# The third-weight output of two token groups as one Strassen step, transposed, instead of two plain accumulations

## The chip, the cores and the metric

One core of a Trainium2 chip runs the whole program in one launch. The metric is the device time of that launch in microseconds. Engines: TensorE (PE) multiplies 128x128 stationary blocks by moving blocks of up to 512 columns into PSUM, VectorE (DVE), ScalarE (ACT) and GpSimd (POOL) do the elementwise work, SyncE (SP) issues most DMAs.

## The reference

Two batches of 768 tokens with 8 heads of 64 pass through a decayed linear attention, then through two feed-forward blocks, all in float32:

```python
x = attn_out.transpose(0, 2, 1, 3).reshape(1536, 512)
h = x @ w_in                       # 512 -> 2048
x = np.maximum(0.01 * h, h) @ w_out   # 2048 -> 512
a = x @ w1                         # 512 -> 1024
b = x @ w2                         # 512 -> 1024
out = ((a * b) @ w3) @ w_out2      # 1024 -> 1024 -> 512
```

## The kernel before, in words

The 1536 tokens form three groups of 512 (`T`, `NG`). Each float32 operand of a product is split into a rounded high half and the rest (`hi` on ScalarE, `lo` on VectorE or GpSimd, both in `halves_of`, L821), and each product is three matmuls (`EXACT`: high-high, low-high, high-low). `w3` and the last weight are multiplied with each other first (`unit_w`, L1044); the result `w34` (1024 x 512, eight slices of 128 rows) is kept in two float32 tiles. This is the "third weight" of the title.

The last part of the program works on eight slices of the inner dimension F (1024 = 8 x 128). For the first group, `unit_ab` makes a slice of a*b and `unit_o` (L1280) multiplies it by its slice of `w34`. For the second and third group together, `unit_pair` (L964) makes a and b of a slice by one Strassen step: seven products of 6 matmuls each (p1 to p7, L981) into three PSUM banks, with copies on ScalarE (`keep`, L993) and adds and multiplications on VectorE (`dve`, L997) between them. The operands that come from the weights are made for each slice in `pair_weights` (L930): four 256-wide sums and four splits. The results: m0 is a*b of the second group, m1 that of the third. m0 is split at once (`pair_ops`, L691); m1 is stored and split later (`stored_pair`, L1035).

The output of those two groups is plain. `unit_o(1, f)` runs between the products of the next pair, `unit_o(2, f)` after the last pair. In each, for 4 chunks of 128 tokens, the chunk of a*b is the stationary operand and the slice of `w34` (512 columns) the moving one, three products each, accumulated over the eight slices (`accumulate`, L728, matmuls at L689, banks `acc` for the second group, `ps` for the third). The pieces of `w34` are split anew for each group, in the ring `wy`. At the end each 128 x 512 result is copied to a tile `f` and stored; the very last copy is done in two halves by VectorE and ScalarE.

The order of all engines is fixed when the program is built. `in_order` (L65) holds every operation with a cost, a rank, what it comes after and which buffers it takes and uses; each time an engine is free it gives it the operation of lowest rank among those that are ready. A buffer belongs to a ring of a few slots (`RINGS`), and a take waits for the users of the slot's former owner. An operation with `port=True` on VectorE and any on GpSimd are never planned at the same time. `both` (L834) is one elementwise operation of VectorE or GpSimd on two SBUF operands, `WIDE` for 512 columns.

Of the kernel before, what the change touches and what calls it, by code (L numbers as in the profile page):

```python
# [20 lines left out]
T = 512  # L21
# [103 lines left out]
def tile_kernel(ctx: ExitStack, tc, qkv, lamb, w_in, w_out, w1, w2, w3t, wo, out):  # L125
# [4 lines left out]
    RINGS = {  # L130
# [3 lines left out]
    }  # L134

    TAGS = {"yf0": ("yf0",), "yf1": ("yf1",), "yf2": ("yf2",)}
# [1 line left out]
    TAGS["sd"] = ("wide0", "wide1", "more0", "more1")  # L138
    TWO = {
        "sx": (("w34_4", "w34_5"), ("w34_6", "w34_7"), ("old0", "old1"), ("old2", "old3")),  # L140
        "wy": tuple((f"w34_{2 * i}", f"w34_{2 * i + 1}") for i in range(4)),
    }
    FIXED = (
        "raw", "rp", "rn", "u", "f", "wi", "wp", "wx", "xy", "inp", "act", "qd", "kd", "a", "yf0", "yf1", "yf2", "sx",
        "wy", "sd",
    )
    pools = {
        r: ctx.enter_context(tc.tile_pool(name=r, bufs=n, **({"space": PS} if r in ("ps", "acc") else {})))
# [12 lines left out]
    def new(buf, shape, dtype=F32):  # L161
        tags = TAGS.get(buf.ring, (buf.ring,))
        turn[buf.ring] = turn.get(buf.ring, -1) + 1
        if buf.ring in TWO:
            tags = TWO[buf.ring][turn[buf.ring] % 4]
# [158 lines left out]
    def weight(kind, i, g, rank):  # L324

        if (kind, i) in pairs:
            return pairs[kind, i]
        if kind == "w34":
            get, last, fb = (lambda: w34[i // 4][:, i % 4, :]), kept_op[kind, i], []
        elif (kind, i) in kept_op:  # L330
            get, last, fb = (lambda: kept[i].tile[int(kind == "w2")]), kept_op[kind, i], [kept[i]]
        else:
            get, last, fb = convert(kind, i, rank)
            if kind in ("w1", "w2"):
                kept_op[kind, i] = last
        two = kind == "w34" and g > 0
        buf = Buf("wy" if two else "wi" if kind == "in" or kind == "wo" and i < 6 else "wp")
# [3 lines left out]
        if two and g == 1 and i < 4:  # L341
            order += kept[i].users

        def split(e):
            new(buf, [P, 512] if two else [P, 2, 512], F32R)
            hi(lambda: part(0), get)(e)

        part = (lambda v: buf.tile[v]) if two else (lambda v: buf.tile[:, v, :])
# [3 lines left out]
        o2 = op(  # L352
            {"dve": 680} if len(pairs) < 4 else {"dve": 680, "pool": 1250}, lo(lambda: part(1), lambda: part(0), get),
            rank, [o1], [],
            [*fb, *takes, *uses], port=True,
        )
        if kind in ("in", "out"):
# [4 lines left out]
    wo_buf, wo_part = {}, {}  # L362

# [359 lines left out]
        gp[g, f] = pair_ops(o1, ps, rank_next)  # L723

    yf, yf_ops, ys, y_ops = {}, {}, {}, {}
    held = []

    def accumulate(tag, g, f, nf, rank, w_ops, bufs, job, pairs, evac):  # L728

        if f % nf == 0:  # L730
            accs[tag, g] = [Buf("ps" if tag == "o" and g == NG - 1 else "acc") for _ in range(4)]
        acc = accs[tag, g]
        first = f % nf == 0
        after = [*w_ops, *([] if first else [acc_op[tag, g]])]
# [6 lines left out]
                products([(acc[c].tile, *job(c)) for c in cs], pairs, first, last)  # L741
            return fn

        if tag == "o" and g == NG - 1 and f == nf - 2:

            held.append((after, bufs, job))
            return
        if first and g == NG - 1:
            for c in range(4):
                after.append(op({"pe": 680}, mm([c], False), rank, after, [acc[c]], bufs, behind=after[-1:]))  # L750
            acc_op[tag, g] = after[-1]
            return
        if tag == "o" and g == 1 and f == nf - 2:
            for k in range(2):
                after.append(op({"pe": 1360}, mm([2 * k, 2 * k + 1], False), rank + 16 * k, after, [], [*acc, *bufs]))
            acc_op[tag, g] = after[-1]
            return
        if f % nf < nf - 1:
# [4 lines left out]
        two = [*held] if tag == "o" else []  # L763
        for after2, bufs2, _ in two:
            after, bufs = [*after, *after2], [*bufs, *bufs2]
        for c in range(4):
            def steps_of(e, c=c, fn=mm([c], True)):
                for _, _, job2 in two:
                    products([(acc[c].tile, *job2(c))], pairs, False, False)
                fn(e)  # L770

            o = op({"pe": 680 * (1 + len(two))}, steps_of, rank, after, [], [acc[c], *bufs])
            evac(c, acc[c], o)

    def unit_y(g, f, rank):
# [183 lines left out]
        quarters(("a22",), w2f(1), [last], w, n)  # L959
        return st  # L960

    stored, through, store_buf = {}, {}, {}

    def unit_pair(f, rank):  # L964

# [34 lines left out]
                takes, uses,  # L1000
            )

        p1 = product(0, b1, "a11", "b11", [], through[f - 1][:1] if f else ())
        t1, s1 = keep("ta", b1, p1)
        p7 = product(5, b3, "s3", "t3", [], through[f - 1] if f else ())
        p6 = product(10, b1, "s2", "t2", [p1, s1])
# [4 lines left out]
        t4, k4 = keep("ta", b1, p5)  # L1011
        r22 = Buf("tb")
        c22 = dve(lambda: new(r22, [P, T]), lambda: b3.tile, lambda: t4.tile, ALU.add, [p7, k4], [r22], [b3, t4])
        p3 = product(35, b1, "s4", "b22", [p5, k4])

        if f % 2 == 0:
            store_buf[f // 2] = Buf("wi")
        sb = store_buf[f // 2]

        def store():  # L1020
            if f % 2 == 0:
                new(sb, [P, 2, T])
            stored[f] = sb.tile[:, f % 2, :]
            return stored[f]

        m1 = dve(store, lambda: b1.tile, lambda: r22.tile, ALU.mult, [p3, c22], [] if f % 2 else [sb], [b1, r22, *([sb] if f % 2 else [])])
        p4 = product(40, b3, "a22", "t4", [p7, c22])
        through[f] = p2, p3, p4
        r21 = Buf("ta")
        c21 = dve(lambda: new(r21, [P, T]), lambda: b3.tile, lambda: u2.tile, ALU.add, [p4, k2], [r21], [b3, u2])  # L1030
        m0 = dve(lambda: b2.tile, lambda: b2.tile, lambda: r21.tile, ALU.mult, [c11, c21], [], [b2, r21])
        abp[1, f] = pair_ops(m0, b2, soon)
        kept_op["ab", f] = m1

    def stored_pair(f, rank):  # L1035

        buf = Buf("act")
        ops_ = halves_of(
            lambda v: buf.tile[:, v, :], lambda: stored[f], [kept_op["ab", f]], [buf], [store_buf[f // 2]], rank,
            lambda: new(buf, [P, 2, T], F32R),  # L1040
        )
        abp[2, f] = buf, ops_

    def unit_w(f, rank, rank_next):  # L1044
        halves = [weight("w3", 2 * f + j, 0, rank) for j in range(2)]
# [234 lines left out]
    def unit_o(g, f, rank):  # L1280
# [4 lines left out]
        def evac(c, acc, o):  # L1285
            fb = Buf("f")
            r0 = g * T + c * P

            def fn(e):
                copy = nc.scalar.copy if e == "act" else nc.vector.tensor_copy  # L1290
                copy(new(fb, [P, DM]), acc.tile)

            if g == NG - 1 and c == CPG - 1:

                def part(k):
                    def half_fn(e):
                        if k == 0:
                            new(fb, [P, DM])
                        copy = nc.scalar.copy if e == "act" else nc.vector.tensor_copy
                        w = slice(k * DM // 2, (k + 1) * DM // 2)  # L1300
                        copy(fb.tile[:, w], acc.tile[:, w])  # L1301
                        (nc.scalar if k else nc.sync).dma_start(out=out[r0 : r0 + P, w], in_=fb.tile[:, w])
                    return half_fn

                op0 = op({"dve": 300}, part(0), rank, [o], [fb], [acc])
                op({"act": 300}, part(1), rank, [o], [], [acc, fb], behind=[op0])
                return
# [77 lines left out]
        unit_o(0, f, r(f) + 20)  # L1385
    rank = r(NF2)
    pair_late(rank - 40)
    r = lambda f: rank + 45 * f
    for f in range(NF2):
        if f == NF2 - 1:  # L1390
            stored_pair(0, r(f))
        unit_pair(f, r(f))
        if f:
            unit_o(1, f - 1, r(f) + 25)
    unit_o(1, NF2 - 1, r(NF2) + 15)
    for f in range(NF2):
        if f:
            stored_pair(f, r(NF2) + 10 * f)
        unit_o(2, f, r(NF2) + 20 + 10 * f)

    with tc.manual_schedule():
        for o, e in in_order(ops, RINGS, FIXED):
# [58 lines left out]
```

## Time and profile before

| | |
|---|---|
| median of 3 runs | 537.4 us (537.16 to 539.24) |
| profiled execution, its time | 538.08 us |
| its span, first to last instruction | 536.4 us |
| granted TensorE clock, mean | 0.998 |
| busy in the span: PE, DVE, ACT, POOL | 524.2, 379.2, 330.1, 129.1 us |
| first product of a pair, last matmul's end | 406.97 us, 531.89 us |

The span is the part of the execution that the profile shows; the time is 1.7 us more. An engine's busy time says how much of the span it works, and the chain that ended last says which of them set the end.

### The profile page before, as it was taken

How to read it: one execution, taken by the hardware profiler on the slowest of the kernel's cores; microseconds unless marked ns; L12 is line 12 of the kernel's file. 1: busy time of each engine (PE TensorE's matmuls, PEld its weight loads, DVE VectorE, ACT ScalarE, POOL GpSimd, SP SyncE). 2: the span in 40 equal slices, each digit the busy share in tenths (PEclk: the TensorE clock that was granted, in tenths of full speed). 3: DMA queues.
4: the chain of work that ended last, by engine and by line, in shares of the span. 5: the costliest groups of instructions: out<-in, count | busy, mean ns of one | idle time of the engine just before them, and what ended most of it. 6: DMA issues, size and time to landing. Idle time of an engine off the chain costs nothing.

```text
span 536.4 us, 8563 instructions
## 1 busy us (share of the span) xinstructions
PE 524.2 (98%) x3340; PEld 431.9 (81%) x3340; DVE 379.2 (71%) x623; ACT 330.1 (62%) x611; POOL 129.1 (24%) x114
## 2 busy tenths in 40 slices
PE   5999899999999999999999999999999999999996
PEld 5788788888888888888888888888888888888885
DVE  6987596989879538749566799998986555443450
ACT  5998795649775536745674667868655444342352
POOL 2312041322522102220242130300113543330110
PEclk9999999999999999999999999999999999999999
DMA  8985651104242111322312334446102000000022
GB/s 309 412 297 192 248 159 42 39 2 158 80 155 93 65 40 46 112 78 77 119 61 97 117 112 127 155 131 198 64 1 78 1 0 1 0 0 2 0 79 79
DMA packets 15880, 54.03 MB, mean 101 GB/s; under 512 B 1888, under 2 KB 2144, under 8 KB 15840
## 3 DMA queue, kind: packets, MB, share of 16 engines
q1 hardware_dynamic: 15552, 53.35, 28.9%
q8 instruction: 26, 0.43, 0.3%
q10 hardware_dynamic: 288, 0.14, 0.1%
q14 instruction: 14, 0.11, 0.1%
HBM read 50.34 MB, written 3.15 MB: 100 GB/s over the span
## 4 chain that ended last, share of the span: by engine, by line
PE 97%; DMA 1%; issue 0%; ACT 0%; SPq 0%; DVE 0%
PE acc L689 33%; PE ps L682 21%; PE ps L981 14%; PE ps L1191 11%; PE ps L1057 8%; PE ps L689 4%; PE ps L591 3%; PE acc L399 2%; DMA yf<-in_qkv_dram 1%; PE ps L399 1%; PE ps L671 1%; SPq L389 0%; ACT xy L508 0%; DVE f L1301 0%; ACT f L1301 0%
## 5 line engine op out<-in xcount | busy, mean ns | idle before, releaser
L689 PE MATMUL acc<-act,wp 128*128 128x512 f32 x396 | 96.1, 391 | 0.0
L689 PEld LDWEIGHTS acc<-act,wp 128*128 128x128 f32 x396 | 74.0, 188 | 15.6
L682 PE MATMUL ps<-xy,wi 128*128 128x512 f32 x288 | 69.7, 392 | 0.7 <-ACT xy L508 0.7
L277 ACT ACTIVATE rp<-raw,bp 128x512 f32<-128x512 uint16 x72 | 55.1, 766 | 14.0 <-DVE f L303 12.2
L682 PEld LDWEIGHTS ps<-xy,wi 128*128 128x128 f32 x288 | 53.6, 188 | 12.6 <-ACT xy L508 0.9
L277 ACT ACTIVATE rn<-raw,bn 128x512 f32<-128x512 uint16 x72 | 54.4, 762 | 10.2 <-DVE rp L281 7.2
L281 DVE SCALAR_TENSOR_TENSOR rp<-rp,rn 128x512 uint32<-128x512 f32 x72 | 51.4, 713 | 3.2 <-ACT rn L277 2.4
L179 DVE TENSOR_TENSOR act<-ps,act 128x512 fp32r<-128x512 f32 x52 | 35.6, 685 | 14.8 <-ACT act L697 14.6
L682 PE MATMUL ps<-xy,wp 128*128 128x512 f32 x192 | 45.6, 389 | 0.0
L303 DVE SCALAR_TENSOR_TENSOR f<-rp,u 128x512 uint32<-128x512 uint32 x56 | 43.4, 777 | 2.5 <-POOL wi L179 1.3
L689 PE MATMUL acc<-act,wx 128*128 128x512 f32 x180 | 43.7, 390 | 0.0
L682 PEld LDWEIGHTS ps<-xy,wp 128*128 128x128 f32 x192 | 36.0, 188 | 7.5
L689 PEld LDWEIGHTS acc<-act,wx 128*128 128x128 f32 x180 | 33.7, 188 | 7.1
L697 ACT CAST act<-ps 128x512 fp32r<-128x512 f32 x52 | 30.5, 586 | 11.3 <-PE acc L689 7.7
L287 DVE TENSOR_SCALAR u<-raw 128x512 uint32<-128x512 uint32 x72 | 34.1, 478 | 2.7 <-DMA raw<-in_w_out_dram 2.6
L981 PE MATMUL ps<-xy,raw 128*128 128x512 f32 x144 | 34.9, 396 | 0.0
L1057 PE MATMUL ps<-wi,wp 128*128 128x512 f32 x144 | 34.9, 389 | 0.0
L981 PE MATMUL ps<-xy,wp 128*128 128x512 f32 x144 | 34.0, 390 | 0.0
L981 PEld LDWEIGHTS ps<-xy,raw 128*128 128x128 f32 x144 | 27.0, 188 | 6.6 <-ACT ta L995 0.3
L981 PEld LDWEIGHTS ps<-xy,wp 128*128 128x128 f32 x144 | 27.0, 188 | 5.7
L1057 PEld LDWEIGHTS ps<-wi,wp 128*128 128x128 f32 x144 | 27.0, 188 | 5.6
L718 ACT ACTIVATE ps<-ps 128x512 f32<-128x512 f32 x24 | 14.0, 582 | 22.5 <-PE ps L682 22.3
(209 smaller groups left out, 987.8 us busy)
## 6 DMA issues: line engine op xcount, KB each, us to landing
raw<-in_w_in_dram SPq DMA_DIRECT2D x16, 512.0 KB, 4.7
raw<-in_w_out_dram SPq DMA_DIRECT2D x16, 512.0 KB, 4.0
raw<-in_w3t_dram SPq DMA_DIRECT2D x16, 512.0 KB, 3.5
raw<-in_w_dram SPq DMA_DIRECT2D x16, 512.0 KB, 3.3
yf<-in_qkv_dram SPq DMA_DIRECT2D x14, 512.0 KB, 6.6
inp<-in_qkv_dram SPq DMA_DIRECT2D x10, 512.0 KB, 9.5
raw<-in_wo_dram SPq DMA_DIRECT2D x8, 512.0 KB, 3.3
out_dram<-f SPq DMA_DIRECT2D x11, 256.0 KB, 2.0
```

The source lines that it names most:

```text
L179: engines[e].tensor_tensor(out=dst(), in0=src(), in1=hi_().bitcast(F32), op=ALU.subtract)
L277: nc.scalar.activation(out=new(buf, [P, 512]), in_=top, func=AF.Relu, scale=8.0, bias=T_[bias])
L281: nc.vector.scalar_tensor_tensor(out=rp.tile.bitcast(U32), in0=rp.tile, scalar=32768.0, in1=rn.tile, op0=ALU.min, op1=ALU.add)
L287: nc.vector.tensor_scalar(out=new(u, [P, 512], U32), in0=mid, scalar1=2.0**-13, scalar2=2.0**19 - 1, op0=ALU.mult, op1=ALU.min)
L303: nc.vector.scalar_tensor_tensor(out=get().bitcast(U32), in0=rp.tile.bitcast(U32), scalar=16, in1=u.tile, op0=ALU.logical_shift_left, op1= ...
L399: nc.tensor.matmul(*args, start=start, stop=True, skip_group_check=True)
L682: nc.tensor.matmul(o, w(a)[:, cc * P : (cc + 1) * P], x(b, cc), start=k == 0, stop=k == 3 * NCC - 1)
L689: nc.tensor.matmul(o, st(a), mv(b), start=first and k == 0, stop=last and k == 2)
L697: nc.scalar.copy(buf.tile[:, 0, :], ps.tile)
L981: nc.tensor.matmul(ps.tile, w(a, kk), mv(b, kk), start=fresh and kk == 0 and i == 0, stop=kk == NCC // 2 - 1 and i == 2, skip_group_check= ...
L1057: nc.tensor.matmul(ps.tile, w(a)[:, k * P : (k + 1) * P], wo_part[j](b), start=j == 0 and n == 0, stop=j == NF2 - 1 and n == 2,)
L1191: nc.tensor.matmul(ps.tile, w(a, kk), mv(b, kk), start=fresh and kk == 0 and i == 0, stop=kk == NCC // 2 - 1 and i == 2, skip_group_check= ...
```

## The change

The output of the second and third group becomes one matrix product, transposed: (512 columns x 1024) times (1024 x 1024 tokens of both groups), and it is done by one Strassen step that halves all three dimensions: the columns of the output (2 x 256), the F slices (0 to 3 and 4 to 7) and the groups. `w34` is the stationary operand, a*b the moving one. Each of the seven products has 2 column blocks of 128, 4 slices and 3 matmuls. m0 and m1 of a pair are written over the weights of that slice (`kept`) as plain float32. The sums of `w34` quarters are made in place or in two tiles `f`, those of a*b in place or in four tiles `sd`; every operand of a product is then split into halves. The pairs follow each other at a rank distance of 35 instead of 45, the first product of a pair has its rank lowered by 10. The output of these groups is stored transposed, and the host turns it when it collects the result. `unit_o` stays for the first group; `wy`, `stored_pair` and the special cases of the third group in `accumulate` go.

The diff, cut to its core:

```diff
-        "sx": 4, "wy": 4, "sd": 4, "kp": 8,
+        "sx": 4, "sq": 2, "sd": 4, "kp": 8,
...
-        if tag == "o" and g == NG - 1 and f == nf - 2:
-
-            held.append((after, bufs, job))
-            return
...
-        p1 = product(0, b1, "a11", "b11", [], through[f - 1][:1] if f else ())
+        p1 = product(-10, b1, "a11", "b11", [], through[f - 1][:1] if f else ())
...
-        p3 = product(35, b1, "s4", "b22", [p5, k4])
...
+        p3 = product(30, b1, "s4", "b22", [p5, k4])
+        ab = kept[f]
+        read = [*ab.users]
+        m1 = dve(lambda: ab.tile[1], lambda: b1.tile, lambda: r22.tile, ALU.mult, [p3, c22, *read], [], [b1, r22])
+        p4 = product(35, b3, "a22", "t4", [p7, c22])
         through[f] = p2, p3, p4
         r21 = Buf("ta")
         c21 = dve(lambda: new(r21, [P, T]), lambda: b3.tile, lambda: u2.tile, ALU.add, [p4, k2], [r21], [b3, u2])
-        m0 = dve(lambda: b2.tile, lambda: b2.tile, lambda: r21.tile, ALU.mult, [c11, c21], [], [b2, r21])
-        abp[1, f] = pair_ops(m0, b2, soon)
-        kept_op["ab", f] = m1
-
-    def stored_pair(f, rank):
-
-        buf = Buf("act")
-        ops_ = halves_of(
-            lambda v: buf.tile[:, v, :], lambda: stored[f], [kept_op["ab", f]], [buf], [store_buf[f // 2]], rank,
-            lambda: new(buf, [P, 2, T], F32R),
+        m0 = dve(lambda: ab.tile[0], lambda: b2.tile, lambda: r21.tile, ALU.mult, [c11, c21, *read], [], [b2, r21])
+        ab_op[f] = m0, m1
+
+    ab_op = {}
+    def unit_out(rank, early):
+
+        n, h = NF2 // 2, DM // 2
+        quarters = {"a11": (0, 0), "a21": (0, 1), "a12": (1, 0), "a22": (1, 1)}
+
+        def w(name, u):
+            half, col = quarters[name]
+            return lambda: w34[half][:, 2 * u : 2 * u + 2, col * h : (col + 1) * h]
+
...
+        b11, b12 = (lambda t: (lambda: kept[t].tile[0])), (lambda t: (lambda: kept[t].tile[1]))
+        b21, b22 = (lambda t: (lambda: kept[t + n].tile[0])), (lambda t: (lambda: kept[t + n].tile[1]))
+        x = [Buf("sd") for _ in range(n)]
+        nothing = lambda u: []
+        stationary("a11", "wx", lambda u: w("a11", u), lambda u: w34_read, nothing, rank - 100)
+        stationary("a12", "sq", lambda u: w("a12", u), lambda u: w34_read, nothing, rank - 90)
+        free = lambda name, u: left[name, u][1]
+        done = {}
+        for u in range(2):
+            s1_ops.append(
+                both(
+                    lambda u=u: s1[u].tile.rearrange("p (t n) -> p t n", n=h), w("a21", u), w("a22", u), ALU.add,
+                    w34_read, rank - 95, WIDE, [s1[u]], [], lambda u=u: new(s1[u], [P, 2 * h]),
+                )
+            )
+            done["s3", u] = both(
+                w("a21", u), w("a11", u), w("a21", u), ALU.subtract, [s1_ops[u], *w34_read], rank - 94, WIDE
+            )
+            done["s2", u] = both(
+                w("a11", u), lambda u=u: s1[u].tile.rearrange("p (t n) -> p t n", n=h), w("a11", u), ALU.subtract,
+                [s1_ops[u], done["s3", u], *free("a11", u)], rank - 93, WIDE, [], [s1[u]],
+            )
+            done["s4", u] = both(
+                w("a12", u), w("a12", u), w("a11", u), ALU.subtract, [done["s2", u], *free("a12", u)], rank - 92, WIDE
+            )
+        t1, t2, t3, t4 = {}, {}, {}, {}
+        for t in range(n):
+            moving_part("b11", t, "wi", b11(t), [ab_op[t][0]], [], early(t))
+            t1[t] = both(
+                b11(t), b12(t), b11(t), ALU.subtract, [*ab_op[t], *right["b11", t][1]], early(t) + 1, WIDE
+            )
+        for t in range(n):
+            at = early(t + n)
+            moving_part("b21", t, "act" if t < 3 else "wp", b21(t), [ab_op[t + n][0]], [], at - 20 if t < n - 1 else rank - 70)
+            t2[t] = both(
+                lambda t=t: x[t].tile, b22(t), b11(t), ALU.subtract, [ab_op[t + n][1], t1[t], *m_ops["t4"]], at, WIDE,
+                [x[t]], [], lambda t=t: new(x[t], [P, T]),
+            )
+            t3[t] = both(
+                b12(t), b22(t), b12(t), ALU.subtract, [ab_op[t + n][1], t1[t]], at + 1, WIDE
+            )
+            t4[t] = both(
+                b21(t), b21(t), lambda t=t: x[t].tile, ALU.subtract, [t2[t], *right["b21", t][1]], at + 2, WIDE, [],
+                [x[t]],
+            )
+        stationary("s2", "raw", lambda u: w("a11", u), lambda u: [done["s2", u], done["s4", u]], nothing, rank - 15)
+        for t in range(n):
+            ring = "raw" if t < 2 else "wp"
+            moving_part("t2", t, ring, lambda t=t: x[t].tile, [t2[t]], [x[t]], rank + 2 * t)
+        stationary("s3", "wx", lambda u: w("a21", u), lambda u: [done["s3", u]], nothing, rank + 18)
+        for t in range(n):
+            moving_part("t3", t, "xy", b12(t), [t3[t]], [], rank + 20 + 2 * t)
+        stationary(
+            "s1", "act", lambda u: (lambda: s1[u].tile.rearrange("p (t n) -> p t n", n=h)), lambda u: [s1_ops[u]],
+            lambda u: [s1[u]], rank + 38,
         )
-        abp[2, f] = buf, ops_
+        for t in range(n):
+            moving_part("t1", t, "xy", b11(t), [t1[t], t2[t]], [], rank + 40 + 2 * t)
+        stationary("a22", "raw", lambda u: w("a22", u), lambda u: [s1_ops[u]], nothing, rank + 58)
+        for t in range(n):
+            moving_part("t4", t, "xy", b21(t), [t4[t]], [], rank + 60 + 2 * t)
+        stationary("s4", "raw", lambda u: w("a12", u), lambda u: [done["s4", u]], nothing, rank + 78)
+        for t in range(n):
+            moving_part("b22", t, "wi", b22(t), [t2[t], t3[t]], [], rank + 80 + 2 * t)
+
...
+                    for t in range(n):
+                        wl, mv = left[a, t // 2][0], right[b, t][0]
+                        for i, (v, v2) in enumerate(EXACT):
+                            nc.tensor.matmul(
+                                ps.tile, wl(v, t, c), mv(v2), start=start and t == 0 and i == 0,
+                                stop=t == n - 1 and i == 2, skip_group_check=True,
+                            )
...
+                o = op(
+                    {"pe": 2720}, fn, rank + k + 10 * c, [*ready, *(after[c] if after else [])], [ps] if start else [],
+                    [*bufs, *([] if start else [ps])], last_pe[-1:],
+                )
...
+        pair = lambda k: [[o] for _, o in k]
+        q1 = product(0, 1, "a11", "b11", [], True)
+        k1 = keep("tb", 1, q1)
+        q2 = product(20, 2, "a12", "b21", [], True)
+        finish(0, 1, 2, q2, k1)
+        q6 = product(40, 1, "s2", "t2", pair(k1), False)
+        k2 = keep("tb", 1, q6)
+        q7 = product(60, 3, "s3", "t3", [], True)
+        q5 = product(80, 1, "s1", "t1", pair(k2), False)
+        k4 = keep("ta", 1, q5)
+        e22 = finish(1, 2, 3, q7, k4)
+        q4 = product(100, 3, "a22", "t4", [[o] for o in e22], False)
+        finish(1, 1, 3, q4, k2)
+        q3 = product(120, 1, "s4", "b22", pair(k4), False)
...
-    r = lambda f: rank + 45 * f
+    r = lambda f: rank + 35 * f
     for f in range(NF2):
-        if f == NF2 - 1:
-            stored_pair(0, r(f))
         unit_pair(f, r(f))
-        if f:
-            unit_o(1, f - 1, r(f) + 25)
-    unit_o(1, NF2 - 1, r(NF2) + 15)
-    for f in range(NF2):
-        if f:
-            stored_pair(f, r(NF2) + 10 * f)
-        unit_o(2, f, r(NF2) + 20 + 10 * f)
+    unit_out(r(NF2), lambda f: r(f) + 60)
...
+    o = r.results[0]["out_0_dram"]
+    return np.concatenate([o[:T], *(o[g * T : (g + 1) * T].T for g in range(1, NG))])
```

`nothing` stands for "no users"; `stationary` makes two split pieces of a quarter of `w34` in a ring, `moving_part` one split slice of a*b, `keep` copies both banks of a product on ScalarE, `finish` adds a bank to a kept result on VectorE into `f` and stores 128 rows of the transposed output. The last product's two banks are each copied in two halves, as the last one was before.

## Rows read from the trace of the kernel before

**Rows 1.** The page, busy time of TensorE and granted clock in 40 slices.
```profile
PE 524.2 (98%) x3340; PEld 431.9 (81%) x3340; DVE 379.2 (71%) x623; ACT 330.1 (62%) x611; POOL 129.1 (24%) x114
...
PEclk9999999999999999999999999999999999999999
```
**Rows 2.** The chain that ended last, from 330 us: start, us, what.
```profile
398.81 5.44 PE ps L682 x24
...
411.10 15.29 PE ps L981 x66
426.39 2.79 PE acc L689 x12
429.19 9.73 PE ps L981 x42
438.92 2.78 PE acc L689 x12
...
501.15 1.39 PE acc L689 x6
...
506.67 2.10 PE ps L689 x9
508.77 2.80 PE acc L689 x12
511.57 20.32 PE ps L689 x87
...
531.91 0.43 DVE f L1301
...
532.37 0.37 ACT f L1301
```
**Rows 3.** Windows: us, then PE, PEld, DVE, ACT, POOL busy, clock, DMA.
```profile
406.97:531.89 124.92, 124.91 (x541) 100.99 (x539) 58.93 (x88) 50.23 (x90) 34.09 (x34) 1.00 0.06 22
...
340.00:400.00 60.00, 60.00 (x266) 49.68 (x265) 55.61 (x94) 43.28 (x73) 12.30 (x8) 1.00 0.31 102
```
**Rows 4.** Waits of TensorE's weight loads, 406 to 536 us (all).
```profile
PEld ps L981 <- ACT ta L995: 0.3, 1, 0.3
```
**Rows 5.** Matmuls of L981 and L1191 by operands (moving, stationary): ns min/median/max.
```profile
L981 PE MATMUL ps<-xy,raw x144: 388/394/498, 410.9 to 493.9; 128*128 128x512 f32 x144
...
L981 PE MATMUL ps<-xy,wp x144: 389/389/397, 420.8 to 504.9; 128*128 128x512 f32 x144
```
```profile
L1191 PE MATMUL ps<-xy,sx x36: 390/394/404, 140.8 to 280.1; 128*128 128x512 f32 x36
```
**Rows 6.** VectorE by form, 406.8 to 512 us: busy, mean ns, idle before.
```profile
L999 DVE TENSOR_TENSOR ps<-ps,ta 128x512 f32<-128x512 f32 x16 | 11.2, 699 | 15.2 <-PE ps L981 15.0
...
L999 DVE TENSOR_TENSOR wi<-ps,yf 128x512 f32<-128x512 f32 x8 | 5.5, 691 | 3.5 <-PE ps L981 3.2
...
L179 DVE TENSOR_TENSOR raw<-rp,raw 128x512 fp32r<-128x512 f32 x3 | 2.1, 692 | 4.1 <-ACT raw L175 4.1
...
L838 DVE TENSOR_TENSOR rp<-rp,inp 128x256 f32<-128x256 f32 x4 | 1.7, 421 | 0.8 <-POOL rp L838 0.8
...
L179 DVE TENSOR_TENSOR xy<-x,xy 128x512 fp32r<-128x512 f32 x1 | 1.5, 1539 | 0.0
```
**Rows 7.** All engines by form, 380 to 537 us.
```profile
L995 ACT COPY ta<-ps 128x512 f32<-128x512 f32 x16 | 9.4, 585 | 12.9 <-PE ps L981 12.6 <-ACT ta L995 0.3
...
L179 POOL TENSOR_TENSOR raw<-rn,raw 128x512 fp32r<-128x512 f32 x3 | 3.9, 1296 | 8.4 <-ACT raw L175 8.4
...
L175 ACT CAST raw<-rp 128x512 fp32r<-128x512 f32 x4 | 2.5, 622 | 4.0 <-PE ps L981 2.3 <-DVE rp L838 1.7
...
L1301 DVE COPY f<-ps 128x256 f32<-128x256 f32 x1 | 0.4, 423 | 7.1 <-PE ps L689 7.1
```
**Rows 8.** Line L838, 512-wide sums on VectorE: ns min/median/max.
```profile
L838 DVE TENSOR_TENSOR ta<-ta,xy x12: 676/680/1791, 92.5 to 117.1; 128x512 f32<-128x512 f32 x12
```
**Rows 9.** The page, issues of output DMAs: KB each, us to landing.
```profile
out_dram<-f SPq DMA_DIRECT2D x11, 256.0 KB, 2.0
```

More of the change, by code (lines that the diff above doesn't have):

```diff
@@ L140, in tile_kernel @@
         "sx": (("w34_4", "w34_5"), ("w34_6", "w34_7"), ("old0", "old1"), ("old2", "old3")),
-        "wy": tuple((f"w34_{2 * i}", f"w34_{2 * i + 1}") for i in range(4)),
+        "sq": (("old0", "old1"), ("old2", "old3")),
     }
@@ L144, in tile_kernel @@
         "raw", "rp", "rn", "u", "f", "wi", "wp", "wx", "xy", "inp", "act", "qd", "kd", "a", "yf0", "yf1", "yf2", "sx",
-        "wy", "sd",
+        "sq", "sd",
     )
@@ L164, in new @@
         if buf.ring in TWO:
[L165 removed]
+            tags = TWO[buf.ring][turn[buf.ring] % len(TWO[buf.ring])]
             buf.tile = [const.tile(shape, dtype, tag=tag, name=buf.ring) for tag in tags]
@@ L335, in weight @@
                 kept_op[kind, i] = last
-        two = kind == "w34" and g > 0
-        buf = Buf("wy" if two else "wi" if kind == "in" or kind == "wo" and i < 6 else "wp")
+        buf = Buf("wi" if kind == "in" or kind == "wo" and i < 6 else "wp")
         if kind == "out" and i % 3 == 1 or kind == "wo" and i >= 6:
@@ L340, in weight @@
         takes, uses, order = [buf], [], [last]
-        if two and g == 1 and i < 4:
-            order += kept[i].users
         def split(e):
-            new(buf, [P, 512] if two else [P, 2, 512], F32R)
+            new(buf, [P, 2, 512], F32R)
             hi(lambda: part(0), get)(e)
-        part = (lambda v: buf.tile[v]) if two else (lambda v: buf.tile[:, v, :])
+        part = lambda v: buf.tile[:, v, :]
         if kind == "wo":
@@ L356, in weight @@
         )
+        if kind == "w34":
+            w34_read.extend([o1, o2])
         if kind in ("in", "out"):
@@ L360, in weight @@
         return part, [o1, o2], buf
-    wo_buf, wo_part = {}, {}
+    wo_buf, wo_part, w34_read = {}, {}, []
     xs, x_ops = {}, {}
@@ L725, in tile_kernel @@
     yf, yf_ops, ys, y_ops = {}, {}, {}, {}
-    held = []
     def accumulate(tag, g, f, nf, rank, w_ops, bufs, job, pairs, evac):
         if f % nf == 0:
-            accs[tag, g] = [Buf("ps" if tag == "o" and g == NG - 1 else "acc") for _ in range(4)]
+            accs[tag, g] = [Buf("acc") for _ in range(4)]
         acc = accs[tag, g]
@@ L750, in accumulate @@
                 after.append(op({"pe": 680}, mm([c], False), rank, after, [acc[c]], bufs, behind=after[-1:]))
[L751 to L755, printed above, removed]
             acc_op[tag, g] = after[-1]
@@ L762, in accumulate @@
             return
-        two = [*held] if tag == "o" else []
-        for after2, bufs2, _ in two:
-            after, bufs = [*after, *after2], [*bufs, *bufs2]
         for c in range(4):
[L767 to L772, printed above, removed]
+            o = op({"pe": 680}, mm([c], True), rank, after, [], [acc[c], *bufs])
             evac(c, acc[c], o)
@@ L960, in pair_weights @@
         return st
-    stored, through, store_buf = {}, {}, {}
+    through = {}
     def unit_pair(f, rank):
@@ L1013, in unit_pair @@
         c22 = dve(lambda: new(r22, [P, T]), lambda: b3.tile, lambda: t4.tile, ALU.add, [p7, k4], [r22], [b3, t4])
-        p3 = product(35, b1, "s4", "b22", [p5, k4])
[L1016 to L1027, printed above, removed]
+        p3 = product(30, b1, "s4", "b22", [p5, k4])
[3 more added lines that the diff above has]
+        p4 = product(35, b3, "a22", "t4", [p7, c22])
         through[f] = p2, p3, p4
@@ L1291, in fn @@
                 copy(new(fb, [P, DM]), acc.tile)
[L1293 to L1307, printed above, removed]
             o1 = op({"act": 500, "dve": 602}, fn, rank, [o], [fb], [acc])
@@ L1459 @@
     r = run_bass_kernel_spmd(nc, [arrays], core_ids=[0])
-    return r.results[0]["out_0_dram"]
+    o = r.results[0]["out_0_dram"]
+    return np.concatenate([o[:T], *(o[g * T : (g + 1) * T].T for g in range(1, NG))])
```

101 lines of the change are left out of this document (added).

## The prediction

> **What bounds the kernel now.** I read the page first. TensorE is busy for 98% of the span and its clock is granted in full in every slice [rows 1], so only fewer or faster matmuls can shorten the kernel; VectorE (71%) and ScalarE (62%) matter only where they make TensorE wait. Next comes the chain that ended last [rows 2]: through the stretch that the change rewrites it is TensorE alone, the products of `unit_pair` (L981) alternating with the output products of the second group (L689, acc), then those of the third (L689, ps), and at the very end two small copies and a DMA. The waits confirm it: from 406 us on, TensorE's weight loads waited once, for 0.3 us [rows 4]. The windows [rows 3] say how loaded the others are there: in the 124.92 us from the first pair product to the last matmul VectorE works 58.93, ScalarE 50.23 and GpSimd 34.09 us. Between 340 and 400 us VectorE was at 55.61 of 60 (93%), and TensorE never stopped. So a busy VectorE does not by itself stall this schedule.
>
> **What the change removes on TensorE.** Each of the eight F slices has 4 token chunks times 3 products for each of two groups: 8 x 12 x 2 = 192 matmuls. Their time stands in [rows 2]. The second group has six blocks like 2.79 and 2.78, two halves of 1.39 and one of 2.80: 22.29 us. The third: 2.10 + 20.32 = 22.42 us. Together 44.71 us, 233 ns a matmul.
>
> **What it adds there.** Seven products, each 2 column blocks x 4 slices x 3 = 24: 168 matmuls of the same shape. Their rate is one of two that the trace shows. The first is 5.44 us for 24 (227 ns), where the pieces are of the plain rings; the second is the 233 ns above. The same split shows in the durations: with the stationary operand in `wp` 389 ns, in `raw` 394, and from an `xy` moving tile with `sx` weights (the constant tiles) 394 [rows 5]. By that, a11 (`wx`), s3 (`wx`), s1 (`act`) and half of s2 x t2 (both in `raw`) should be quick, a12 (`sq`, the tiles of `sx`), a22 and s4 (`raw`) and the other half of s2 slow: 84 at 227 and 84 at 232 ns (2.79 / 12) = 38.5 us. Saving 6.2 us. Bounds: 168 x 232.5 = 39.1 (saving 5.6) and 168 x 226.7 = 38.1 (saving 6.6). I take 6.2.
>
> **What it costs elsewhere.** Counting from the code, with durations from [rows 6 to 8]:
> - Removed: 32 hi/lo splits (second group's result, stored third group, output weights twice) and eight evacuations, of which VectorE had three (0.69) and a half.
> - Added: 42 splits (7 stationary matrices in 2 pieces, 7 moving in 4) and 24 sums of 512 columns. A lo half is 0.69 us on VectorE or 1.30 on GpSimd, a 512-wide sum 0.68 (median). Six results more are kept by ScalarE (0.59 each) and six added by VectorE (0.69); the last two are cut in halves as the last one was (0.42 and 0.37).
> - VectorE and GpSimd together: 58.93 plus what GpSimd carried, 34.09 us x 0.69/1.30 = 18.1, is 77.0 us in VectorE's measure. Minus 22.1 (32 x 0.69) and 2.1, plus 66 x 0.69 = 45.5, 6 x 0.69 = 4.1 and 0.4: 102.8 us. TensorE will need 124.9 - 6.2 = 118.7. If VectorE did it all alone it would be 87% busy, less than the 93% between 340 and 400 us.
> - ScalarE: 50.2 + 10 x 0.62 + 6 x 0.59 - 5 x 0.59 + 0.4 = 57, far from 118.7.
> - Output DMAs: four 256 KB rows of the first group, then six whole and four halves, the same bytes as now; nothing else is on SP's queue then, and one lands in 2.0 us [rows 9]. The tail after the last matmul stays: half copy, half copy, DMA, 4.5 us from 531.9 to 536.4. The last but one result leaves 12 matmuls before the end instead of 6. Nothing.
>
> So the added work hides under TensorE in sum; the question is whether it hides at each place.
>
> **Pair stage.** The output products of the second group, 12 matmuls, were TensorE's filler between the fifth and third product of a pair; they go. In their place the change moves the next pair's first product there (rank -10), 6 matmuls or 1.39 us. What hides in it is the copy of p5 (0.59) ahead of p3. The sum c22 (0.69) has p3 as well, another 1.39: 1.28 of work under 2.78. Then the seventh product of the next pair reuses the bank that m1 reads: m1 (0.69) hides under p4 (1.39), and if another VectorE operation of 0.69 has just begun, 1.38 under 1.39. The trace has a test: in the 66 matmuls from 411.10 us there is no filler at all, and the stretch took 15.29 us, 231.7 ns each, with the single wait of 0.3 us. So per pair between 0 and 0.3, and I take 0 to 0.1: 0.3 us for the eight. High end 2.4.
>
> **Hand-over.** At the end of the last pair, p4's result goes through c21 and m0 (0.69 each), the hi half (0.62) and the lo half (0.69, or 1.30 on GpSimd) before q2 can use the last slice of b21: 2.7 to 3.3 us. Cover: q1 is ready early; each of its halves is 2.8 us. Its first half probably goes out as filler before p3, which leaves the second: 2.8. If both go out earlier, only the 9 matmuls of q2 on the slices 0 to 2 (2.1 us) lie between. Cost 0 to 1.2; I take 0.4. Behind it q6 waits for t2, and each later product for 10 to 12 vector operations; six products of 5.5 us give 33 us for at most 32 splits and sums (22 us), six adds (4.1) and the last pair's results (2).
>
> Sum: -6.2 + 0.3 + 0.4 = -5.5 us. The profiled execution took 538.08 us (span 536.4), 0.7 over the median of 537.4; its own time would become 532.6 and the median 531.9.
>
> **A rule that speaks against it.** VectorE and GpSimd get in each other's way: one lo half that meets a GpSimd operation took 1.54 us instead of 0.69 [rows 6], and of the 512-wide sums the longest took 1.79 where the median is 0.68 [rows 8]. The Trainium skill ("SBUF — State Buffer", section "Who interferes with whom") says that a VectorE instruction with two SBUF inputs and a GpSimd one that reads SBUF exclude each other, the second blocked for the whole of the first. The trace agrees as far as these rows go, and all 66 added operations are of that kind. By the rule at its hardest the sum is that of the first rival; by the row of 93% it stays -5.5.
>
> **The rivals.**
> 1. *Contention eats the gain.* Every operation given to GpSimd saves VectorE on average 0.53 us (18.1/34 operations) but may block it for 0.85 (1.54 - 0.69). With x blocked meetings VectorE needs 102.8 + 0.32x and passes 118.7 at x = 50; GpSimd ran 34 there. With all 66 it needs 124, 5 us too many, and the time would be about 537. For it: the share of two-input operations grows. Against it: GpSimd held 34 operations in this stretch and TensorE waited once.
> 2. *The hand-over and the pair stage both stall at their high ends*: 2.4 + 1.2, so 534.8 to 535. For it: TensorE's products of the output are in a fixed order, so nothing else can fill. Against it: the 0.3 us of [rows 4].
> 3. *Slower: the preparation is not done ahead.* The sums and splits have late ranks; if only the six splits of q1 are ready at the last pair's end, 60 x 0.69 + 4.1 + 1.4 = 46.9 us of VectorE must fit before q3 starts, 33 us later: a stall of 13.9, and 537.4 - 6.2 + 13.9 = 545. It passes +0.5% when fewer than about 7 operations are done ahead. Against it: the planner gives an idle engine any ready operation whatever its rank, 34 are ready before that point (weights as soon as the first group's output is done, slices 0 to 6 with their pairs), and VectorE has some 2 us to spare in each pair (5 x 0.69 + 4 x 0.42 + 3.5 x 0.69 = 7.6 of 9.7), with GpSimd beside it.
>
> **How the numbers follow.** This measurement can tell about 0.5%, 2.7 us, from no change. Forecast, stalls under 2.2 us (530.4 to 534): 0.66. Rival 1 in part or whole: 0.15, of which a third is still below 534.7. Rival 2: 0.12, half of it below 534.7. Rival 3: 0.07. Faster 0.66 + 0.05 + 0.06, about 0.77; same 0.16; slower 0.07. The range runs from the saving of 6.6 without any stall, with 0.4 of spread (530.4), to rival 2 and most of rival 1 (536.5).
>
> **What would show it right or wrong.** After: 168 matmuls in place of 192, about 38.5 us; pair blocks of 42 matmuls still 9.6 to 9.7 us; TensorE's waits in the stretch under 1.5 us in all; VectorE near 80 to 85% busy, GpSimd as much as now; the last matmul near 526.4 us and 4.5 us behind it. Wrong, if TensorE waits for VectorE or GpSimd at the start of q2, q6 or q7, if VectorE's splits take well over 0.8 us on average, or if the pair blocks stretch past 10 us.

## The result and the profile after

The changed kernel takes 532.8 us (median of 6 runs, 530.71 to 534.54), the kernel before 537.91 (6 runs): ratio 0.9896, 95% interval 0.9866 to 0.9926, so 1.0% faster. Forecast were 531.9 and 530.4 to 536.5. The profiled execution has a span of 531.8 us and took 533.54.

The page's busy time and clock, answering to [rows 1]:

```profile
PE 519.0 (98%) x3316; PEld 426.8 (80%) x3316; DVE 404.3 (76%) x658; ACT 336.4 (63%) x623; POOL 136.9 (26%) x118
...
PEclk9999999999999999999999999999999999999999
```

There are 24 matmuls fewer (3316 against 3340), VectorE works 25 us more, and TensorE, at 98%, is still the engine that sets the end. The chain that ended last, answering to [rows 2] (L961 is the pair's product, L1143 the output's; start, us, what):

```profile
407.70 1.40 PE ps L961 x6
409.10 2.73 PE acc L687 x12
411.83 9.84 PE ps L961 x42
...
428.92 1.19 DVE wp L179 x2
430.12 0.61 DVE yf L979
430.73 0.04 issue
430.77 56.09 PE ps L961 x240
486.87 2.72 PE acc L1143 x12
489.58 2.72 PE ps L961 x12
492.31 13.90 PE acc L1143 x60
506.20 5.44 PE ps L1143 x24
511.64 5.45 PE acc L1143 x24
517.09 5.60 PE ps L1143 x24
522.69 5.58 PE acc L1143 x24
...
528.29 0.44 DVE f L1215
```

The reader sees three things. The output product now takes 2.72 + 13.90 + 5.44 + 5.45 + 5.60 + 5.58 = 38.69 us instead of 44.71. The chain no longer stays on TensorE through the pairs: between 421.7 and 430.8 us it runs over VectorE, with one ScalarE operation in it. And the last matmul is followed by 3.53 us (528.27 to 531.8) instead of 4.51. The waits of the weight loads from 400 us on, answering to [rows 4] (us in total, times, longest):

```profile
PEld ps L961 <- ACT ta L975: 1.8, 7, 0.3
PEld ps L961 <- DVE yf L979: 1.3, 2, 1.2
```

A load runs ahead of its matmul, so these 3.1 us are not all lost: where the longest load waited 1.2 us, the matmuls behind it stood still for 0.74 (shown below).

The issue that lands last, on ScalarE's queue (KB, us to landing), before and after:

```profile
out_dram<-f ACTq DMA_DIRECT2D x1, 128.0 KB, 2.6
```

```profile
out_dram<-f ACTq DMA_DIRECT2D x2, 128.0 KB, 1.7
```

The span is 4.6 us shorter, and it splits without a rest:

| part | before | after | difference | forecast |
|---|---|---|---|---|
| start to the first pair product | 406.97 | 407.70 | +0.73 | 0 |
| output product | 44.71 | 38.69 | -6.02 | -6.2 |
| pairs and all their waits (stretch minus output product minus one first-group block of 2.73) | 77.48 | 79.15 | +1.67 | +0.7 with the hand-over |
| last matmul to the end | 4.51 | 3.53 | -0.98 | 0 |

The first line is no effect of the change: in the runs below the first pair product stands anywhere from 405.49 to 408.91 us, with the same program up to there in some of them. That is why the experiments are compared by the **stretch** from the first pair product to the last matmul, read off the chain of one profiled execution each: 124.92 us before, 120.57 after. Where two kernels do the same, its pieces agree to 0.1 us (the 240 matmuls of the pairs took 56.09 us here and 56.03 in e1); a ratio of times stands beside it.

### The profile page after: what moved, and what is told of

Same layout as the page of the kernel before. It is cut to its first block, busy times and chain, and to the rows that moved or that the text cites. A ratio compares the mean times of both kernels' runs of the same rounds, so it can differ in the third digit from the quotient of the medians.

```text
span 531.8 us, 8582 instructions
## 1 busy us (share of the span) xinstructions
PE 519.0 (98%) x3316; PEld 426.8 (80%) x3316; DVE 404.3 (76%) x658; ACT 336.4 (63%) x623; POOL 136.9 (26%) x118
## 4 chain that ended last, share of the span: by engine, by line
PE 96%; DVE 2%; DMA 1%; issue 0%; ACT 0%; SPq 0%
PE acc L687 29%; PE ps L680 21%; PE ps L961 13%; PE ps L1369 11%; PE ps L1235 8%; PE acc L1143 5%; PE ps L589 3%; PE ps L1143 2%; PE acc L397 2%; DMA yf<-in_qkv_dram 1%; PE ps L397 1%; PE ps L669 1%; DVE w L818 0%; DVE rp L818 0%; DVE wi L179 0%
## 5 line engine op out<-in xcount | busy, mean ns | idle before, releaser
L179 DVE TENSOR_TENSOR act<-ps,act 128x512 fp32r<-128x512 f32 x44 | 30.1, 685 | 9.0 <-ACT act L695 8.8
L961 PE MATMUL ps<-xy,wp 128*128 128x512 f32 x144 | 34.7, 393 | 0.7 <-DVE yf L979 0.7
L961 PE MATMUL ps<-xy,raw 128*128 128x512 f32 x144 | 35.1, 397 | 0.0
L961 PEld LDWEIGHTS ps<-xy,wp 128*128 128x128 f32 x144 | 26.7, 188 | 7.5 <-DVE yf L979 1.2
L695 ACT CAST act<-ps 128x512 fp32r<-128x512 f32 x44 | 25.8, 585 | 10.8 <-PE acc L687 7.7
L961 PEld LDWEIGHTS ps<-xy,raw 128*128 128x128 f32 x144 | 26.7, 188 | 7.2 <-ACT ta L975 1.1
```

The costliest lines, as they stand in the source:

```text
L179: engines[e].tensor_tensor(out=dst(), in0=src(), in1=hi_().bitcast(F32), op=ALU.subtract)
L695: nc.scalar.copy(buf.tile[:, 0, :], ps.tile)
L961: nc.tensor.matmul(ps.tile, w(a, kk), mv(b, kk), start=fresh and kk == 0 and i == 0, stop=kk == NCC // 2 - 1 and i == 2, skip_group_check= ...
```

## The experiments

Each changes one thing in the changed kernel unless it says otherwise.

| run | stretch, us | time, us (runs) | ratio to the kernel before, 95% |
|---|---|---|---|
| before | 124.92 | | |
| after | 120.57 | 532.8 (6) | 0.9896 [0.9866, 0.9926] |
| e1_extra24 | 126.09 | 538.13 (10) | 0.9996 [0.9969, 1.0023] |
| e2_w34_dve | 119.45 | 531.66 (4) | 0.9868 [0.9835, 0.9901] |
| e3_copy_first | 118.87 | 531.82 (4) | 0.9870 [0.9834, 0.9906] |
| e4_raw_pad | 120.19 | 530.13 (4) | 0.9832 [0.9791, 0.9873] |
| e5_raw_128 | 120.25 | 531.73 (4) | 0.9883 [0.9849, 0.9916] |
| b1_before_raw128 | 123.36 | 535.51 (10) | 0.9957 [0.9934, 0.9980] |
| e9_copy_raw128 | 118.25 | 529.14 (5) | 0.9832 [0.9803, 0.9860] |
| e6_late_prep | 138.08 | 550.4 (1) | |
| e7_sums_pool | 119.88 | 532.13 (1) | |

**Is it the count of matmuls?** One product is made twice:

```diff
-                    for t in range(n):
...
+                    reps = 2 if a == "a12" else 1
+                    for rep in range(reps):
+                        for t in range(n):
```

(and the planner's cost of that product is doubled)

> The product a12 x b21 is computed twice into the same bank, 24 matmuls more, so TensorE has 192 again and the output is not the reference's. Theory (the gain is the 24 matmuls that fell away, nothing else): 24 x 232 ns = 5.6 us more than the changed kernel, a span near 537.4 and a time near 538, level with the kernel before. Rival (part of the gain comes from the new order of the tail and part of the 24 would hide in TensorE's waits): 2 to 4 us more, a time of 535 to 537.

The stretch grew by 5.52 us and the ratio is 1 within 0.3%: the gain is gone. Its chain has 84 matmuls in 19.47 us where the changed kernel has 60 in 13.90:

```profile
493.46 19.47 PE acc L1145 x84
```

All 24 count in full (232 ns each); none hides in a wait. The theory holds.

**Where the pair stage lost 1.67 us, first part: the wait of 1.2 us.** The 42 matmuls of the second pair take 10.8 us (421.50 to 432.26) where the others take 9.7 to 9.9. The timeline of the changed kernel there (start, us, engine, what, idle before and releaser):

```profile
421.50 5.63 PE L961 MATMUL ps<-xy,wp 128*128 128x512 f32 x24
...
423.15 1.48 POOL L818 TENSOR_TENSOR w<-w,w 128x512 f32<-128x512 f32 x1
...
423.80 1.37 DVE L179 TENSOR_TENSOR wi<-w,wi 128x512 fp32r<-128x512 f32 x1 [0.33 <-ACT wi L175]
...
424.59 1.74 POOL L179 TENSOR_TENSOR sq<-w,sq 128x512 fp32r<-128x512 f32 x1
425.10 1.52 DVE L818 TENSOR_TENSOR rp<-rp,inp 128x256 f32<-128x256 f32 x1
...
426.41 1.36 POOL L818 TENSOR_TENSOR w<-w,w 128x512 f32<-128x512 f32 x1
426.54 1.78 DVE L818 TENSOR_TENSOR w<-w,w 128x512 f32<-128x512 f32 x1
...
430.04 0.68 DVE L979 TENSOR_TENSOR yf<-ps,ta 128x512 f32<-128x512 f32 x1
...
430.77 1.65 PE L961 MATMUL ps<-xy,wp 128*128 128x512 f32 x6 [0.74 <-DVE yf L979]
```

Three VectorE operations in a row take 1.37, 1.52 and 1.78 us instead of 0.69, 0.42 and 0.68 [rows 6, 8], 2.9 us more, each beside a GpSimd operation and each ending 0.3 to 0.6 us after it. Behind them in VectorE's queue stand an add and two splits and then c22 (430.04, result in yf), the sum for which p4 waits. The Trainium skill ("SBUF — State Buffer", section "Who interferes with whom") says that a VectorE operation with two SBUF operands and a GpSimd operation that reads SBUF exclude each other. The trace agrees in these three. Here three of the added operations (two sums of `w34` and the split of a12) are GpSimd's part.

```diff
-                w("a21", u), w("a11", u), w("a21", u), ALU.subtract, [s1_ops[u], *w34_read], rank - 94, WIDE
+                w("a21", u), w("a11", u), w("a21", u), ALU.subtract, [s1_ops[u], *w34_read], rank - 94, {"dve": 680}
...
+                    {"dve": 680} if name in ("a11", "a12") else None,
```

(and so for all four kinds of `w34` sums; the second line is a new argument of `halves_of`)

> The eight sums of the w34 quarters and the splits of a11 and a12 are planned on VectorE alone, so GpSimd no longer runs them early in the pair stage. Theory (the wait of TensorE near 430 us, 1.2 us for the weight load and 0.7 for the matmul, comes from VectorE operations that were blocked by GpSimd ones: lo 1.37 us, narrow sum 1.52, wide sum 1.78 instead of 0.69, 0.42 and 0.68): that wait goes, the second pair's 42 matmuls come down from 10.8 to 9.7 us, the span falls by 1.0 us. Rival (VectorE has simply too much queued there): the operations that move to VectorE add some 2 us of work at that place, the wait stays or grows to 2 us and more, the span rises by 0 to 1.5 us.

The wait on yf is gone, the list has only this line left, and the stretch fell by 1.12 us:

```profile
PEld ps L961 <- ACT ta L975: 1.9, 7, 0.3
```

The rival, a longer wait behind a fuller VectorE queue, did not come. But GpSimd took up other operations instead (42.82 us in the stretch against 41.41, VectorE 81.98 against 82.15), and one blocked operation (a split of 1.79 us) still stands ahead of c22. So the run shows that the wait goes with the three-fold pile-up, not that GpSimd should do less.

**Second part: the seven waits of 0.3 us.** In the same timeline, at the end of a fifth product:

```profile
417.45 0.62 ACT L175 CAST raw<-rp 128x512 fp32r<-128x512 f32 x1 [0.77 <-PE ps L961]
417.98 0.58 ACT L975 COPY ta<-ps 128x512 f32<-128x512 f32 x1
...
418.61 2.62 PEld L961 LDWEIGHTS ps<-xy,raw 128*128 128x128 f32 x12 [0.26 <-ACT ta L975]
```

The end of p5 frees a weight slot and makes its result ready at once; ScalarE does the split of later weights first and the copy that p3 waits for second, so the weight load of p3 comes 0.26 us late. (The planner sees a freed buffer without the 60 ns that it adds for a result, so the split wins by rule.)

```diff
-        quarters(("s1", "s2"), lambda: sa.tile, [o2], sa, DM)
+        quarters(("s1", "s2"), lambda: sa.tile, [o2, *copied.get(f - 2, ())], sa, DM)
...
+        copied[f] = [k4]
```

> The split of a pair's s1/s2 weights on ScalarE is planned only after the copy of the fifth product of the pair that used the slot before, so the copy goes first on ScalarE. Theory (the seven waits of 0.2 to 0.3 us on the copy ta come from a 0.62 us split that takes ScalarE in the moment in which the fifth product ends): those waits go, pairs on wp come down to 9.6 and on raw to 9.7 us, the span falls by 0.6 to 0.9 us. Rival (the copy is late for its own 0.58 us and the filler product of 1.4 us is too short): the waits stay at 0.2 us and more, the span moves by less than 0.2.

The waits went; the order on ScalarE is now the other one:

```profile
427.38 0.59 ACT L975 COPY ta<-ps 128x512 f32<-128x512 f32 x1 [0.80 <-PE ps L961]
427.86 0.62 ACT L175 CAST wp<-rp 128x512 fp32r<-128x512 f32 x1
...
428.29 2.69 PEld L961 LDWEIGHTS ps<-xy,wp 128*128 128x128 f32 x12
```

The stretch fell by 1.70 us, more than the 0.6 to 0.9 forecast: the wait on yf at 430 us is gone as well, since the order has shifted and with it what meets what (from 423.96 us to c22 at 428.00 no VectorE operation takes over 0.8 us). So the 1.2 us wait hangs on the exact meeting and need not occur. One wait of 0.3 us is left, as in the kernel before [rows 4], and 120.57 - 118.87 = 1.70 is all of the pair stage's 1.67: some 1.0 from the second pair's wait and 0.1 from each of the seven.

**More on GpSimd: the first rival.** All 24 sums on GpSimd:

```diff
-                b12(t), b22(t), b12(t), ALU.subtract, [ab_op[t + n][1], t1[t]], at + 1, WIDE
+                b12(t), b22(t), b12(t), ALU.subtract, [ab_op[t + n][1], t1[t]], at + 1, {"pool": 1250}
```

(and so for every `both` of the output product)

> The 24 sums of the output product's operands are planned on GpSimd alone (1.30 us each). Theory (meetings of two-operand operations of GpSimd and VectorE cost VectorE time and reach TensorE only where a copy or an add of a pair stands behind one): GpSimd's busy time in the stretch rises from 42 to some 60 us, VectorE's splits get longer on average (over 0.80 us), TensorE's waits grow from 3 to 4 to 8 us, the span to 533 to 537. Rival (VectorE is relieved by 24 x 0.69 = 16 us, and has room for the meetings): the span stays within 0.5 us of the changed kernel or falls.

The two windows of the stretch, the changed kernel's and this one's (us; PE, PEld, DVE, ACT, POOL busy):

```profile
407.70:528.27 120.57, 119.82 (x517) 95.89 (x515) 82.15 (x123) 55.63 (x100) 41.41 (x37) 1.00 0.07 25
```

```profile
406.55:526.43 119.88, 119.87 (x516) 95.95 (x515) 84.02 (x112) 55.41 (x100) 61.12 (x48) 1.00 0.07 25
```

GpSimd's time rose to 61 us as expected, and VectorE's to 84 although it has fewer operations, since some are blocked:

```profile
L179 DVE TENSOR_TENSOR act<-inp,act 128x512 fp32r<-128x512 f32 x3 | 5.2, 1727 | 0.1
```

The waits of TensorE's weight loads:

```profile
PEld ps L961 <- ACT ta L975: 2.0, 7, 0.3
PEld ps L961 <- DVE w L979: 0.4, 1, 0.4
```

They are 2.4 us (3.1 in the changed kernel) where 8 were expected, and the stretch is 0.69 shorter, as the wait on yf did not occur here either. Against e2, which lacks that wait too, the stretch is 0.43 longer; not more than that can be read as the cost of the added meetings. The theory falls by its size. VectorE has 36 of 120 us free. The forecast's first rival priced every meeting as a blocked one: with 48 operations on GpSimd it would have VectorE busy for 102.8 + 0.32 x 48 = 118.2 us, and the window has 84.02.

**Is the work done ahead? The third rival's price.** All preparation but that of a11 and b11 waits for the last pair:

```diff
+        last = [ab_op[NF2 - 1][0]]
...
-                    part, src(u), after(u), [buf], uses(u), rank,
+                    part, src(u), [*after(u), *([] if name == "a11" else last)], [buf], uses(u), rank,
```

(and so for the moving operands and the first sums)

> All sums and splits of the output product but those of a11 and b11 wait until the last pair's m0 is made. Theory (the work ahead is what hides it; third rival of the prediction): VectorE gets 60 operations, 41 us, and some 5 us more to do from then on, where TensorE needs 33 us before the last product: a stall of 12 to 15 us, less what GpSimd takes, so a span of 540 to 546. Rival (there is room enough behind the last pair too, since GpSimd and VectorE share it): under 5 us more, a span below 537.

The stretch grew by 17.51 us. Its chain leaves TensorE for a long row of VectorE operations and comes back at a slower pace:

```profile
490.53 0.70 DVE ta L979
...
491.95 2.40 DVE w L818 x4
...
506.45 6.55 PE acc L1144 x16
```

```profile
407.05:545.13 138.08, 126.37 (x517) 99.62 (x515) 83.15 (x130) 55.55 (x100) 37.59 (x31) 0.94 0.06 21
...
500.00:520.00 20.00, 14.07 (x40) 9.54 (x39) 19.64 (x31) 12.41 (x24) 9.89 (x2) 0.67 0.07 26
```

From 500 to 520 us VectorE is busy for 19.64 of 20 us. Over the stretch TensorE is idle for 138.08 - 126.37 = 11.71 us, the changed kernel's for 120.57 - 119.82 = 0.75 (its window stands further up): 11.0 of the 17.5 us are the stall, somewhat less than the forecast's 13.9. The other 6.5 us are pace, which nobody expected and which put the span, 548.7 us, beyond the 540 to 546 that were. In an idle time of 5.77 us, at 498.4 us, the granted clock fell to the lower of its two levels, 1.2 GHz, and stayed there to 512.1; the 16 matmuls from 506.45 took 409 ns each (6.55 / 16) instead of 232. Behind another idle time, of 2.43 us, it was at that level once more from 518.9 to 522.3. In the changed kernel much of this work lies under the pairs: behind 486.87 us VectorE works 23.44 of 41.40 us.

**Where the operands lie.** Slots of `raw` get 28 more 16-bit columns (4160 bytes instead of 4104); the order of every engine stays:

```diff
-            t = new(raw, [P, 4 * 512 + 4], U16)
+            t = new(raw, [P, 4 * 512 + 32], U16)
```

(and so for the other tiles of `raw`)

> The tiles of the ring raw get 28 more 16-bit columns, so that one slot is 4160 bytes and no longer 4104; the order of every engine is the same. Theory (the slower form of matmul, 394 instead of 389 ns, comes from where a tile of raw begins): matmuls with raw weights go to 389 ns, the pairs on raw from 9.8 to 9.7 us, the two products with raw stationary operands from 5.60 to 5.45, the span falls by 168 x 5 ns + 60 x 5 ns = 1.1 us. Rival (it comes from the way in which raw is viewed or filled, or from the neighbours at work): the durations stay at 394 and the span moves by less than 0.2.

Half right. Matmuls that I had not named became quick, those that I had named mostly did not (ns min/median/max). In the changed kernel:

```profile
L1369 PE MATMUL ps<-xy,sx x36: 390/394/404, 141.5 to 280.8; 128*128 128x512 f32 x36
```

```profile
L961 PE MATMUL ps<-xy,raw x144: 388/394/500, 411.7 to 481.0; 128*128 128x512 f32 x144
...
L961 PE MATMUL ps<-wi,raw x24: 390/394/404, 407.5 to 468.3; 128*128 128x512 f32 x24
```

With the wider slots:

```profile
L1369 PE MATMUL ps<-xy,sx x36: 389/389/390, 140.1 to 278.6; 128*128 128x512 f32 x36
```

```profile
L961 PE MATMUL ps<-xy,raw x144: 388/393/496, 409.4 to 478.6; 128*128 128x512 f32 x144
...
L961 PE MATMUL ps<-wi,raw x24: 388/389/389, 405.3 to 466.0; 128*128 128x512 f32 x24
```

The matmuls on the constant tiles (`sx`, `sq`) go to 389 ns with a size that is not theirs. I take it that their places shift with the size of `raw`; the traces do not give the places. Of the 2.7 us by which the time is under the changed kernel's, 0.38 lie in the stretch; the rest lies outside it, above all before the first pair product (405.49 instead of 407.70 us), where the start scatters by as much. A slot of 4224 bytes was to decide whether multiples of 128 count:

```diff
-        T_["ident64"] = const.tile([P, D], F32, name="ident64")
+        T_["ident64"] = const.tile([P, T], F32, tag="more1", name="ident64")[:, :D]
...
-            t = new(raw, [P, 4 * 512 + 4], U16)
+            t = new(raw, [P, 4 * 512 + 64], U16)
```

> The tiles of raw get 60 more 16-bit columns, so that a slot is 4224 bytes, a multiple of 128; a small constant moves into a tile that is free then, to make room; the order of every engine is the same. With 4160 bytes the matmuls with the constant tiles and with the first raw slot had gone to 389 ns and half of the others with raw had stayed at 394. Theory (a matmul is the slower form when the places of its two operands differ by something that is no multiple of 128 bytes): all 168 matmuls with raw weights in the pairs, the 108 with sx and 96 of the output product go to 389 ns, the pairs on raw to 9.6 us plus the wait, the span falls by 372 x 5.4 ns = 2.0 us against the changed kernel. Rival (multiples of 64 count, and the slow half had another reason): as with 4160 bytes, half of the raw matmuls stay at 394, a fall near 1.4.

The theory of multiples of 128 falls: xy with raw stays at 393, and the stretch is the same as with 4160 bytes to 0.1 us.

```profile
L961 PE MATMUL ps<-xy,raw x144: 387/393/496, 410.5 to 479.8; 128*128 128x512 f32 x144
```

The gain within the stretch is 0.3 to 0.4 us. Why those matmuls stay slow is open. The same size in the kernel before:

> The kernel before, with slots of 4224 bytes in raw and nothing else changed. Theory: its 168 raw, 108 sx and 192 wy matmuls all go to 389 ns, 468 x 5.4 ns = 2.5 us less, a span near 533.9; the change is then worth 24 x 227 ns = 5.4 us plus nothing, so part of its gain (0.5 us) was the better place of its operands. Rival (wy keeps its 394, being moving and not stationary): 1.5 us less.

There the matmuls on `wy` all became quick (third group, 19.73 us for 87 instead of 20.32) and the stretch fell by 1.56 us. That is the rival's 1.5, but for the opposite reason: `wy` did become quick, and xy with raw stayed at 393.

```profile
509.64 19.73 PE ps L689 x87
```

With equal slots the output product takes 43.59 us before (16.38 + 2.72 + 2.72 + 2.04 + 19.73) and 38.43 after: the change is worth 5.2 us there, and by this comparison 0.9 of its 6.0 came from tiles that happened to lie better. The whole stretch is then 3.11 us shorter (123.36 against 120.25) and not 4.35.

**Together.** The copy before the split and slots of 4224 bytes:

> The copy before the split on ScalarE, and slots of 4224 bytes. Theory (the two costs are independent): 1.5 us from the first, as it measured between the first pair product and the last matmul, and 2.0 from the second: a span of 528 to 528.6 and some 0.7% less than the changed kernel. Rival (one hides in the other: faster matmuls shorten the cover of the copies): less than 2.5 together.

The stretch is 118.25 us, 2.32 less than the changed kernel's. That is the rival's "less than 2.5" and not the sum of 3.5, but not for the rival's reason: the second part gives 0.3 in the stretch and not 2.0, and 2.32 is even a little more than the two measured alone (1.70 + 0.32), so nothing hides. The time, 529.14 us, is 1.7% under the kernel before, against 1.0% for the change.

## Why the prediction was right

- **TensorE sets the end, and 24 matmuls are the gain.** Right: 38.69 us against 38.5 (the two terms of the forecast, 84 matmuls at either rate, add up to 38.6), and e1, with 24 matmuls more, takes 5.52 us of the gain back. The rates were read well (227 and 232 ns a matmul). Of the pieces, s2 with t2 from `raw` was put down as quick because both lie in one ring; its median was 395 ns.
- **Pair stage.** The step that was mis-sized: "between 0 and 0.3, and I take 0 to 0.1: 0.3 us for the eight" measured 1.67, within its high end of 2.4. Two things are missing in it. It let a copy of 0.59 us hide under 1.39, and did not ask what else the end of that product sets free on ScalarE: a 0.62 us split goes first, the load behind the copy comes 0.3 us late, and each pair pays about 0.1 (e3). And it let c22 start as soon as its copy was done and allowed for one VectorE operation of 0.69 in the way, at m1 only; three blocked ones in a row ahead of c22 cost 1.0 us once (e2).
- **Hand-over.** 0.4 forecast, nothing measured: TensorE does q1's first half at 486.87 ahead of p3 as forecast, and the 60 matmuls from 492.31 run at 231.7 ns, the pace of their operands.
- **The tail** was put at no change and gave 0.98. The last issue, on ScalarE's queue, landed after 1.7 us instead of 2.6. Two things differ ahead of it. The last but one result now leaves from 2.8 us before the last (525.96 and 528.75 us) and not 1.2 (531.12 and 532.36), and it leaves in two issues of 128 KB on two queues, not in one of 256. The forecast had seen the 12 matmuls in between and called them nothing. Which of the two shortens the landing was not tested. The runs that keep the new tail have 3.5 us there too (538.5 - 535.0 in e1, 529.9 - 526.36 in e2), the kernel before with wider slots has 4.3.
- **VectorE.** VectorE's and GpSimd's work together was put at 102.8 us in VectorE's measure; the window above gives 82.15 + 41.41 x 0.53 = 104.1. The "80 to 85% busy" beside it does not follow from that sum: with GpSimd as busy as before it gives (102.8 - 18.1) / 118.7, 71%. Measured were 82.15 of 120.57, 68%, as GpSimd took 41 us and not 34.
- **The signs that it named.** TensorE never waited at the start of q2, q6 or q7, and VectorE's wide splits took 0.78 us on average: as forecast. But the waits were 3.1 us and not under 1.5, one pair block took 10.8 us, past the 10 that it had called wrong, and the last matmul ended at 528.27 us, not near 526.4, with 3.5 us behind it and not 4.5.
- **The rivals.** Contention: seen in single rows, not as a bound (e7). Pair stage and hand-over at their ends: the pair stage came to 1.67 of 2.4 us, the hand-over to none of 1.2. Preparation too late: its price is real (e6: 11.0 us of stall and 6.5 of slower pace), its condition is not met.

The bound and the main term were right by their mechanism. That the sum came out 0.9 us from the median is in part luck: the errors were of about 1 us each and of both signs (+1.0 pairs and hand-over, -1.0 tail, +0.7 start, +0.2 output product), and the tail, which the forecast put at nothing, made good for the pair stage.

## What to carry to other kernels

Where one engine is never free and the others are, count its instructions and take their pace by operand from the trace; the rest of a change is worth what it makes that engine wait, and two windows and the list of its waits show where that is. When an event sets two things free on another engine, ask which goes first: here a filler of 1.4 us covered one operation of 0.6, and not two without a wait. And a blocked pair of VectorE and GpSimd operations cost next to nothing here until something that the bound engine needed stood behind it in the queue.

## What the runs showed of the hardware

The same matmul takes 389 or 394 ns (227 or 232 ns from start to start) and which of the two changed with the size of tiles that it does not touch: growing the slots of another ring by 56 bytes (e4) turned all matmuls on the constant tiles quick, with an unchanged order on every engine. What the rule is stays open; multiples of 128 bytes between slots are not enough (e5). A stall cost more than its idle time: in e6 TensorE was idle for 11.7 us, its granted clock fell to the lower level twice (0.67 in the window from 500 to 520 us), and the slower pace (409 instead of 232 ns a matmul in a row of 16) cost another 6.5 us.
